# A fused linear-attention and MLP kernel on one core: GpSimd work moved out of the first group, rstd of later groups computed on VectorE, first loads regrouped

## Chip, cores, metric

One core of one Trainium2 chip. The metric is the device time of one execution in microseconds (us); lower is better. "Span" is the time from the first to the last instruction in one profiled execution; it is about 1.7 us below the time of that execution (217.1 against 218.81 us before the change). Engine names in profile lines: PE is TensorE (products), PEld its weight loads, DVE is VectorE, ACT is ScalarE, POOL is GpSimd, SP starts the loads. The granted clock is the share of the full TensorE clock that the profile shows as granted; 1.00 is full.

## The reference

```python
xn  = layernorm(x)                       # x: 2048 tokens x 640, bf16, eps 1e-5
q,k,v = split(xn @ wqkv)                 # 32 heads of 20
pq,pk = phi(q), phi(k)                   # phi(t) = where(t>0, t+1, exp(t)) + 1e-6
kv, z = einsum(pk, v), sum(pk)           # per head
A = (pq @ kv) / (pq @ z + 1e-6) @ wo
B = gelu(xn @ w1 + b1) @ w2 + b2         # 1536 hidden
out = x + A + B
```

## The kernel before

The 2048 tokens are worked on as four groups of four tiles of 128. For each group the kernel makes K (4 tiles), Q (5 products of 128x512 each) and the MLP's hidden layer h (12 products of 128x512, with GELU on ScalarE). The transposes of the next group's normalised tiles stand between the last h products. After the last group come the attention sums and, from about 140 us on, one long run of output products. The instruction order is the written order.

All products take their result space from one rotating pool of eight PSUM banks. A bank comes free only when ScalarE or VectorE has read it. So a late reader stops TensorE eight banks later: in the profile below the sixth, seventh and eighth h products, eight banks after the last three Q tiles, wait 0.33, 1.10 and 1.06 us for VectorE.

```python
def emit_rstd(t0, t1):                   # on ScalarE; profile before: no table load from 2.08 to 28.60 us
    r = rstd[:, t0:t1]
    nc.scalar.activation(out=r, in_=mv[:, t0:t1, 1], func=ACT.Ln, bias=eps_t[:], scale=1.0)
    nc.scalar.activation(out=r, in_=r, func=ACT.Exp, scale=-0.5)

def phi(dst, ps, shaped):                # every K and Q tile goes through this
    e = etmp.tile([P, TOK], BF16, name="e")
    nc.scalar.activation(out=e[:], in_=ps[:], func=ACT.Exp)
    nc.vector.tensor_scalar(out=e[:], in0=e[:], scalar1=1.0, scalar2=1e-6, op0=ALU.min, op1=ALU.add)   # "clamp"
    nc.vector.scalar_tensor_tensor(out=dst, in0=shaped(ps), scalar=0.0, in1=shaped(e), op0=ALU.max, op1=ALU.add)

# ... in emit_Kphi, when the fourth K tile of group g is done:
            for u in range(max(1, g * TPG), (g + 1) * TPG):        # GpSimd sums K over the tokens
                nc.gpsimd.tensor_tensor(out=..., in0=..., in1=pk[:, u, :], op=ALU.add)
            if g == 0:
                emit_masks()                                       # GpSimd builds constant masks
# ...
nc.vector.tensor_copy(out=b1col[:], in_=b1_bf[:])                  # the "b1 cast"
for g in range(NG):
    if g > 0:
        nc.scalar.preload_act_table_set("natural_log_exp_and_others")
        for i in range(TPG): emit_K(g * TPG + i)
    for m in range(NC):
        if g == 0 and m > 0:
            emit_stats(TPG + m - 1)                                # statistics of group 1
        emit_Q(g, m)
    if g < NG - 1:
        emit_rstd((g + 1) * TPG, (g + 2) * TPG)
        for j in range(NJ):                                        # NJ = 12
            emit_h(g, j)
            if 4 <= j < 8:  emit_norm((g + 1) * TPG + j - 4)
            if 8 <= j < 12:
                emit_T((g + 1) * TPG + j - 8, on_act=NC)           # transposes of group g+1
                if g < NG - 2:
                    emit_stats((g + 2) * TPG + j - 8)              # statistics two groups ahead
```

Of the kernel before, what the change touches and what calls it, by code (L numbers as in the profile page):

```python
# [9 lines left out]
ALU = mybir.AluOpType  # L10
BF16 = mybir.dt.bfloat16
F32 = mybir.dt.float32


@with_exitstack
def kernel(
# [12 lines left out]
    nc = tc.nc  # L29
    P = nc.NUM_PARTITIONS  # L30
# [3 lines left out]
    S, D = x2d.shape  # L34
# [3 lines left out]
    NT = S // P  # L38
    NC = D // P
    NJ = F // P  # L40
    TOK = 512
    NG = S // TOK
    TPG = TOK // P
    EPS = 1e-5
    HALF = D // 2
# [27 lines left out]
    zsum = GT[:, NC - 1, :]  # L73
# [13 lines left out]
    Em4 = consts.tile([P, D], BF16, name="Em4")  # L87
    ones = consts.tile([P, 1], BF16, name="ones")
    Z3t = consts.tile([P, NC, H], BF16, name="Z3t")
    eps_t = consts.tile([P, 1], F32, name="eps_t")  # L90
    recT = consts.tile([P, TOK], BF16, name="recT")
    warm = hT[0][:, 0, :]
# [2 lines left out]

    def bank(dtype=F32):
        return psum.tile([P, TOK if dtype == F32 else 2 * TOK], dtype, name="mm", tag="mm")
# [7 lines left out]
    def load_x(t0, t1):  # L105
        nc.sync.dma_start(out=x_all[:, t0:t1, :], in_=xv[:, t0:t1, :])  # L106

    load_x(0, 1)
    load_x(1, 2)
    load_x(2, 3)  # L110
    nc.sync.dma_start(out=wqk[:, :, D : 2 * D], in_=wqkv_v[:, :, D : 2 * D])
    load_x(3, 4)
    nc.sync.dma_start(out=wqk[:, :, 0:D], in_=wqkv_v[:, :, 0:D])
    load_x(4, 8)
    nc.sync.dma_start(out=w1[:], in_=w1_v)
# [54 lines left out]
    def emit_stats(t):  # L170
        emit_stats_half(t, 0)
        emit_stats_half(t, 1)

    def emit_rstd(t0, t1):
        r = rstd[:, t0:t1]
        nc.scalar.activation(out=r, in_=mv[:, t0:t1, 1], func=ACT.Ln, bias=eps_t[:], scale=1.0)
        nc.scalar.activation(out=r, in_=r, func=ACT.Exp, scale=-0.5)

    def emit_norm(t):
        nc.vector.tensor_scalar(  # L180
            out=xn[:, t, :], in0=x_all[:, t, :], scalar1=mv[:, t, 0:1], scalar2=rstd[:, t : t + 1],
            op0=ALU.subtract, op1=ALU.mult,
        )

    def emit_T(t, on_act):
        pT = bank(BF16)[:, 0:D].rearrange("p (c n) -> p c n", c=NC)
        for c in range(NC):
            nc.tensor.transpose(pT[:, c, :], xn[:, t, c * P : (c + 1) * P], identity[:])  # L188
        dst = xnT[:, :, t * P : (t + 1) * P]
        if on_act > 0:  # L190
            nc.scalar.copy(out=dst[:, 0:on_act, :], in_=pT[:, 0:on_act, :])
        if on_act < NC:
            nc.vector.tensor_copy(out=dst[:, on_act:NC, :], in_=pT[:, on_act:NC, :])

    def phi(dst, ps, shaped):
        e = etmp.tile([P, TOK], BF16, name="e")
# [9 lines left out]

    K_ps = {}

    def emit_Ka(t):
        K_ps[t] = bank()  # L210
        for k in range(NC):
            nc.tensor.matmul(  # L212
                K_ps[t][:], lhsT=xnT[:, k, t * P : (t + 1) * P], rhs=wqk[:, k, D : D + TOK],
                start=(k == 0), stop=(k == NC - 1),
            )

    def emit_Kb(t):
        g, i = divmod(t, TPG)
        if i == 0:
            rest_ps[g] = bank()  # L220
        for k in range(NC):
            nc.tensor.matmul(  # L222
                rest_ps[g][:, i * REST : (i + 1) * REST],
                lhsT=xnT[:, k, t * P : (t + 1) * P], rhs=wqk[:, k, D + TOK : 2 * D],
                start=(k == 0), stop=(k == NC - 1),
            )

    def emit_K(t):
        emit_Ka(t)
        emit_Kb(t)  # L230
        emit_Kphi(t)

    def emit_Kphi(t):
        g, i = divmod(t, TPG)
        phi(pk[:, t, 0:TOK], K_ps.pop(t), lambda a: a[:])
        if i == TPG - 1:
            phi(
                pk[:, g * TPG : (g + 1) * TPG, TOK:D], rest_ps[g],
                lambda a: a[:].rearrange("p (t n) -> p t n", t=TPG),
            )  # L240
            for u in range(max(1, g * TPG), (g + 1) * TPG):
                nc.gpsimd.tensor_tensor(  # L242
                    out=zsum if u == NT - 1 else zacc[:], in0=pk[:, 0, :] if u == 1 else zacc[:],
                    in1=pk[:, u, :], op=ALU.add,
                )
            if g == 0:
                emit_masks()

    def emit_Q(g, m):
        ps = bank()  # L250
# [18 lines left out]

    nc.scalar.preload_act_table_set("natural_log_exp_and_others")  # L270
    emit_warm(10)
    for t in range(2):
        emit_stats(t)
        emit_rstd(t, t + 1)
    emit_norm(0)
    emit_T(0, on_act=NC)
    emit_norm(1)
    emit_stats(2)
    emit_rstd(2, 3)
    emit_T(1, on_act=NC)  # L280
    emit_stats_half(3, 0)
    emit_norm(2)
    emit_stats_half(3, 1)
    emit_rstd(3, 4)
    emit_Ka(0)
    emit_Kb(0)
    emit_T(2, on_act=0)
    emit_norm(3)
    emit_Ka(1)
    emit_Kb(1)  # L290
    emit_T(3, on_act=NC)
    emit_Kphi(0)
    emit_Kphi(1)
    emit_K(2)
    emit_K(3)
    nc.vector.tensor_copy(out=b1col[:], in_=b1_bf[:])
    for g in range(NG):
        if g > 0:
            nc.scalar.preload_act_table_set("natural_log_exp_and_others")
            for i in range(TPG):  # L300
                emit_K(g * TPG + i)
        for m in range(NC):
            if g == 0 and m > 0:
                emit_stats(TPG + m - 1)
            emit_Q(g, m)
        if g < NG - 1:
            emit_rstd((g + 1) * TPG, (g + 2) * TPG)
            for j in range(NJ):
                emit_h(g, j)
                if 4 <= j < 4 + TPG:  # L310
                    emit_norm((g + 1) * TPG + j - 4)
                if 8 <= j < 8 + TPG:
                    emit_T((g + 1) * TPG + j - 8, on_act=NC)
                    if g < NG - 2:
                        emit_stats((g + 2) * TPG + j - 8)

    for t in range(NT):
        nc.gpsimd.tensor_tensor(out=x_all[:, t, :], in0=x_all[:, t, :], in1=b2b[:], op=ALU.add)  # L318
# [110 lines left out]
    for j in range(4 + NC, NJ):  # L429
        emit_h(NG - 1, j)  # L430

    for t in range(NT):
        g, i = divmod(t, TPG)
        osb = late[:, 2 * NC + t % 4, :]
        for half in range(2):
            ns = slice(half * HALF, (half + 1) * HALF)
            ps = bank()
            for j in range(NJ):
                nc.tensor.matmul(  # L439
                    ps[:, 0:HALF], lhsT=hT[g][:, j, i * P : (i + 1) * P], rhs=w2[:, j, ns],  # L440
                    start=(j == 0), stop=False,
                )
            for c in range(NC):
                nc.tensor.matmul(  # L444
                    ps[:, 0:HALF], lhsT=pqT[:, c, t * P : (t + 1) * P], rhs=KVW[:, c, ns],
                    start=False, stop=(c == NC - 1),
                )
            nc.vector.tensor_tensor(  # L448
                out=osb[:, ns], in0=ps[:, 0:HALF], in1=x_all[:, t, ns], op=ALU.add
            )  # L450
            if t == NT - 1:
                nc.sync.dma_start(out=ov[:, t, ns], in_=osb[:, ns])
        if t < NT - 1:
            nc.sync.dma_start(out=ov[:, t, :], in_=osb)


# [1 line left out]
_INS = ['A_x', 'A_wqkv', 'A_wo', 'B_x', 'B_w1', 'B_b1', 'B_w2', 'B_b2']  # L458
_OUTS = [((1, 2048, 640), 'bfloat16')]
# [25 lines left out]
```

## Time and profile before

Before the prediction six executions were known: median 219.07 us (218.57 to 220.85).

The page of the profiled execution begins with the span, the busy share of each engine, and the span in 40 slices of 5.4 us; a digit is the busy share in tenths. (Lines of the other engines are left out.)

```profile
span 217.1 us, 3343 instructions
...
PE 208.7 (96%) x1374; PEld 121.8 (56%) x1390; DVE 103.7 (48%) x212; ACT 82.1 (38%) x137; POOL 54.6 (25%) x59
...
PE   7899779999999999999999999999999999999994
...
DVE  4776995399719920595374425812212212112111
```

TensorE is busy nearly everywhere. The gap is in the fifth and sixth slice, 22 to 33 us, where VectorE is full. The timeline of TensorE (start, length, line, operation, operands, count; in brackets the idle time ahead of it and who ended it) shows this gap. Lines left out are busy ones.

```profile
7.37 1.24 PE L212 MATMUL mm<-wqk,xnT 128*128 128x512 bf16 x5 [0.55 <-DMA wqk<-in_A_wqkv_dram]
...
18.80 5.56 PE L262 MATMUL mm<-xnT,w_88 128*128 128x512 bf16 x24
24.69 1.24 PE L262 MATMUL mm<-xnT,w_88 128*128 128x512 bf16 x5 [0.33 <-DVE pqT L201]
27.04 1.24 PE L262 MATMUL mm<-xnT,w_88 128*128 128x512 bf16 x5 [1.10 <-DVE pqT L201]
29.33 2.54 PE L262 MATMUL mm<-xnT,w_88 128*128 128x512 bf16 x10 [1.06 <-DVE pqT L201]
...
36.07 1.24 PE L212 MATMUL mm<-wqk,xnT 128*128 128x512 bf16 x5
```

The first line starts the K products, after waiting 0.55 us for their weights. At 18.80 group 0's h products start. From 24.69 on they stop three times, each time for a bank that VectorE has not yet emptied (line 201 is the second half of phi). The last line is the first K product of group 1. Twelve h products of 1.08 us and four sets of transposes of 0.28 us (both as the chain of waits has them) need 14.08 us; 36.07 - 18.80 is 17.27. So group 0 loses 3.2 us here.

Why VectorE is late, from its own timeline in the same stretch, with ScalarE's and GpSimd's lines below:

```profile
18.55 1.34 DVE L296 CAST b1col<-b_bf 128x12 f32<-128x12 bf16 x1 [1.64 <-DMA b_bf<-in_B_b_dram]
...
20.72 0.88 DVE L166 BATCH_NORM_STATS2 stats<-x_all 128x6 f32<-128x320 bf16 x2
...
25.59 0.66 DVE L198 TENSOR_SCALAR e<-e 128x512 bf16<-128x512 bf16 x1
...
28.59 0.69 DVE L201 SCALAR_TENSOR_TENSOR pqT<-mm,e 128x512 bf16<-128x512 f32 x1
```

```profile
28.05 0.30 ACT L176 ACTIVATE rstd<-mv,eps_t 128x4 f32<-128x4 f32 x1 [4.64 <-DVE mv L168]
...
28.60 1.28 ACT L266 ACT_TABLE_LOAD   x1
29.90 5.31 ACT L266 ACTIVATE hT_80<-mm,b1col 128x512 bf16<-128x512 f32 x9
```

```profile
18.46 2.88 POOL L242 TENSOR_TENSOR zacc<-zacc,pk 128x640 f32<-128x640 f32 x2
```

VectorE waits for b1, then its tiny cast takes 1.34 us: it starts after a GpSimd add (1.40 us each) has begun at 18.46 and ends, at 19.89, as that add ends (19.86). Between Q tiles stand two statistics instructions per tile. A clamp beside GpSimd takes 0.66 us, one alone 0.28. GELU, which frees the first h banks, can start only at 29.90, because rstd and a table load of 1.28 us stand ahead of it.

### The profile page before, as it was taken

Reading aid. Unit: us, or ns where it says so; the run is one execution under the profiler, and the core shown is the slowest. Engines: PE = TensorE matmul, PEld = TensorE weight load, DVE = VectorE, ACT = ScalarE, POOL = GpSimd, SP = SyncE. Lnnn points to the kernel's source line nnn. Section 1 sums busy time; section 2 is a strip of 40 time slices with the busy share of each in tenths; the row PEclk is TensorE's granted clock in tenths of the full one; section 3 lists DMA queues with packets and bytes.
Section 4 is the critical chain, followed back from the end, with each engine's and each line's share of the span. In section 5 each row is a group of like instructions: output and inputs, shape, how many; then the busy total and the mean of one; then the engine's idle time right before and its main releaser. Section 6 shows DMA issues by size and latency. Waiting matters only on the chain.

```text
span 217.1 us, 3343 instructions
## 1 busy us (share of the span) xinstructions
PE 208.7 (96%) x1374; PEld 121.8 (56%) x1390; DVE 103.7 (48%) x212; ACT 82.1 (38%) x137; POOL 54.6 (25%) x59
## 2 busy tenths in 40 slices
PE   7899779999999999999999999999999999999994
PEld 2554335544554445545555565477777777777772
DVE  4776995399719920595374425812212212112111
ACT  3472189959796868751112646500000000000000
POOL 1008860045002700069999800000000000000000
PEclk9999999999999999999999999999999999999999
DMA  5999960000000000000000000001000010010011
GB/s 175 384 363 314 371 239 0 3 2 0 0 3 0 0 0 3 0 0 2 3 0 0 3 2 0 3 18 42 33 30 30 30 63 30 30 33 30 30 63 30
DMA packets 9999, 12.83 MB, mean 59 GB/s; under 512 B 2048, under 2 KB 8960, under 8 KB 9984
## 3 DMA queue, kind: packets, MB, share of 16 engines
q1 hardware_dynamic: 9984, 12.62, 17.1%
q8 instruction: 11, 0.18, 0.4%
q14 instruction: 4, 0.03, 0.0%
HBM read 10.00 MB, written 2.62 MB: 58 GB/s over the span
## 4 chain that ended last, share of the span: by engine, by line
PE 84%; DMA 6%; DVE 5%; SPq 2%; ACT 1%; issue 1%
PE mm L439 24%; PE mm L262 20%; PE mm L444 10%; PE mm L326 8%; PE mm L253 7%; DMA b_bf<-in_B_b_dram 6%; PE mm L212 6%; PE mm L335 2%; PE mm L418 2%; PE mm L222 2%; PE mm L188 2%; DVE stats L166 1%; DVE pqT L201 1%; SPq L106 1%; PE mm L374 1%
## 5 line engine op out<-in xcount | busy, mean ns | idle before, releaser
L262 PE MATMUL mm<-xnT,w_88 128*128 128x512 bf16 x232 | 54.8, 379 | 3.0 <-DVE pqT L201 2.5
L448 DVE TENSOR_TENSOR late<-mm,x_all 128x320 bf16<-128x320 f32 x32 | 15.7, 491 | 58.7 <-PE mm L444 58.7
L262 PEld LDWEIGHTS <-w_88 128*128 128x128 bf16 x240 | 22.8, 98 | 28.8 <-issue 4.1
L242 POOL TENSOR_TENSOR zacc<-zacc,pk 128x640 f32<-128x640 f32 x13 | 18.2, 1398 | 52.4 <-DVE pk L201 51.6
L198 DVE TENSOR_SCALAR e<-e 128x512 bf16<-128x512 bf16 x40 | 18.7, 467 | 24.9 <-ACT e L197 24.9
L197 ACT ACTIVATE e<-mm 128x512 bf16<-128x512 f32 x40 | 23.0, 597 | 15.7 <-DVE pqT L201 5.9
L444 PE MATMUL mm<-late,pqT 128*128 128x320 bf16 x160 | 27.0, 299 | 0.0
L253 PE MATMUL mm<-xnT,wqk 128*128 128x512 bf16 x98 | 22.1, 379 | 0.1
L318 POOL TENSOR_TENSOR x_all<-x_all,b2b 128x640 bf16<-128x640 bf16 x16 | 21.8, 1397 | 0.0
L212 PE MATMUL mm<-wqk,xnT 128*128 128x512 bf16 x77 | 19.6, 379 | 0.7 <-DMA wqk<-in_A_wqkv_dram 0.6
L444 PEld LDWEIGHTS <-pqT 128*128 128x128 bf16 x160 | 15.7, 98 | 6.1
L326 PE MATMUL mm<-pk,xn 128*128 128x512 bf16 x77 | 17.8, 379 | 0.3 <-issue 0.2
L253 PEld LDWEIGHTS <-wqk 128*128 128x128 bf16 x100 | 9.6, 98 | 10.9
L379 DVE TENSOR_TENSOR pqT<-pqT,mm 128x512 bf16<-128x512 bf16 x20 | 12.3, 680 | 6.0 <-PE mm L374 6.0
L166 DVE BATCH_NORM_STATS2 stats<-x_all 128x6 f32<-128x320 bf16 x32 | 13.8, 471 | 2.4 <-DMA x_all<-in_A_x_dram 2.4
L439 PE MATMUL mm<-w_90,hT_82 128*128 128x320 bf16 x96 | 14.3, 299 | 0.0
L439 PE MATMUL mm<-w_90,hT_80 128*128 128x320 bf16 x96 | 14.3, 299 | 0.0
L439 PE MATMUL mm<-w_90,hT_81 128*128 128x320 bf16 x96 | 14.3, 299 | 0.0
L439 PE MATMUL mm<-w_90,hT_1112 128*128 128x320 bf16 x96 | 14.3, 299 | 0.0
L201 DVE SCALAR_TENSOR_TENSOR pk<-mm,e 128x512 bf16<-128x512 f32 x20 | 13.8, 692 | 1.0
L201 DVE SCALAR_TENSOR_TENSOR pqT<-mm,e 128x512 bf16<-128x512 f32 x20 | 13.8, 692 | 0.7
L326 PEld LDWEIGHTS <-xn 128*128 128x128 bf16 x80 | 7.5, 98 | 9.2 <-issue 0.7
(62 smaller groups left out, 198.0 us busy)
## 6 DMA issues: line engine op xcount, KB each, us to landing
out_dram<-late SPq DMA_DIRECT2D x15, 160.0 KB, 1.8
x_all<-in_A_x_dram SPq DMA_DIRECT2D x3, 640.0 KB, 8.4
w_88<-in_B_w_dram SPq DMA_DIRECT2D x1, 1920.0 KB, 13.4
w_90<-in_B_w_dram SPq DMA_DIRECT2D x1, 1920.0 KB, 14.0
wqk<-in_A_wqkv_dram SPq DMA_DIRECT2D x2, 800.0 KB, 6.2
wv<-in_A_wqkv_dram SPq DMA_DIRECT2D x1, 800.0 KB, 9.0
wo<-in_A_wo_dram SPq DMA_DIRECT2D x1, 800.0 KB, 10.5
x_all<-in_A_x_dram SPq DMA_DIRECT2D x4, 160.0 KB, 2.9
```

The lines of the kernel that those rows point to most:

```text
L166: nc.vector.bn_stats(out=st[:, half, :], in_=x_all[:, t, half * HALF : (half + 1) * HALF])
L197: nc.scalar.activation(out=e[:], in_=ps[:], func=ACT.Exp)
L198: nc.vector.tensor_scalar(out=e[:], in0=e[:], scalar1=1.0, scalar2=1e-6, op0=ALU.min, op1=ALU.add)
L201: nc.vector.scalar_tensor_tensor(out=dst, in0=shaped(ps), scalar=0.0, in1=shaped(e), op0=ALU.max, op1=ALU.add)
L212: nc.tensor.matmul(K_ps[t][:], lhsT=xnT[:, k, t * P : (t + 1) * P], rhs=wqk[:, k, D : D + TOK], start=(k == 0), stop=(k == NC - 1),)
L242: nc.gpsimd.tensor_tensor(out=zsum if u == NT - 1 else zacc[:], in0=pk[:, 0, :] if u == 1 else zacc[:], in1=pk[:, u, :], op=ALU.add,)
L253: nc.tensor.matmul(ps[:], lhsT=wqk[:, k, m * P : (m + 1) * P], rhs=xnT[:, k, gs], start=(k == 0), stop=(k == NC - 1),)
L262: nc.tensor.matmul(ps[:], lhsT=w1[:, k, j * P : (j + 1) * P], rhs=xnT[:, k, g * TOK : (g + 1) * TOK], start=(k == 0), stop=(k == NC - 1),)
L318: nc.gpsimd.tensor_tensor(out=x_all[:, t, :], in0=x_all[:, t, :], in1=b2b[:], op=ALU.add)
L326: nc.tensor.matmul(ps[:], lhsT=w, rhs=pk[:, t, 0:TOK], start=(t == 0), stop=(t == NT - 1))
L439: nc.tensor.matmul(ps[:, 0:HALF], lhsT=hT[g][:, j, i * P : (i + 1) * P], rhs=w2[:, j, ns], start=(j == 0), stop=False,)
L444: nc.tensor.matmul(ps[:, 0:HALF], lhsT=pqT[:, c, t * P : (t + 1) * P], rhs=KVW[:, c, ns], start=False, stop=(c == NC - 1),)
```

## The change

The intent was to empty the Q banks of group 0 sooner and to start GELU sooner: no GpSimd work beside VectorE in group 0; the statistics moved behind the Q tiles; rstd of later groups on VectorE, as a Newton iteration on integers and floats, so that GELU's table load need not wait for it; and an earlier start.

```diff
+    def load_wk(k0, k1): ...                       # K weights in two loads
     load_x(0, 1)
-    load_x(1, 2)
-    load_x(2, 3)
-    nc.sync.dma_start(out=wqk[:, :, D : 2 * D], in_=wqkv_v[:, :, D : 2 * D])
-    load_x(3, 4)
+    load_x(1, 4)
+    load_wk(0, 2)
+    load_wk(2, NC)
...
+    def emit_rstd_vector(t0, t1):                  # 13 instructions on 128x4 elements
+        v = mv[...] + EPS; a = v >> 1; y = 0x5F3759DF - a; v = -0.5 * v      # (shortened)
+        for _ in range(3):
+            nc.vector.tensor_tensor(out=a, in0=v, in1=y, op=ALU.mult)
+            nc.vector.tensor_tensor(out=a, in0=a, in1=y, op=ALU.mult)
+            nc.vector.scalar_tensor_tensor(out=y, in0=a, scalar=1.5, in1=y, op0=ALU.add, op1=ALU.mult)
...
-    for t in range(2):
-        emit_stats(t)
-        emit_rstd(t, t + 1)
-    emit_norm(0)
-    emit_T(0, on_act=NC)
+    emit_stats(0)
+    emit_rstd(0, 1)
+    emit_stats_half(1, 0)                          # ahead of norm 0
+    emit_norm(0)
+    emit_T(0, nc.scalar.copy, 0, 3)                # tile 0 in two parts
+    emit_stats_half(1, 1)
+    emit_rstd(1, 2)
+    emit_T(0, nc.scalar.copy, 3, NC)
...
         for m in range(NC):
-            if g == 0 and m > 0:
-                emit_stats(TPG + m - 1)
             emit_Q(g, m)
-        if g < NG - 1:
-            emit_rstd((g + 1) * TPG, (g + 2) * TPG)
-            for j in range(NJ):
-                emit_h(g, j)
-                if 4 <= j < 4 + TPG:
-                    emit_norm((g + 1) * TPG + j - 4)
-                if 8 <= j < 8 + TPG:
-                    emit_T((g + 1) * TPG + j - 8, on_act=NC)
-                    if g < NG - 2:
-                        emit_stats((g + 2) * TPG + j - 8)
+        for j in range(NJ if g < NG - 1 else 0):
+            emit_h(g, j)
+            if g == 0 and j == NJ - 1:             # GpSimd held by a copy that needs the last GELU
+                nc.gpsimd.tensor_copy(out=Z3t[:, 0, 0:1], in_=hT[0][:, j, 0:1])
+                emit_zacc(0)
+                emit_masks()
+            if j < TPG:
+                emit_stats(t1 + j)                 # statistics of the NEXT group, in every group
+            if j == TPG:
+                emit_rstd_vector(t1, t1 + TPG)
+            if TPG <= j < 2 * TPG:
+                emit_norm(t1 + j - TPG)
+            if j > 2 * TPG:
+                emit_T(t1 + j - 2 * TPG - 1, nc.scalar.copy)
+            if j == NJ - 1:
+                emit_T(t1 + TPG - 1, nc.scalar.copy)
...      # the last output piece is cut into 512 and 128 columns instead of 320 and 320
```

More of the change, by code (lines that the diff above doesn't have):

```diff
@@ L12 @@
 F32 = mybir.dt.float32
+I32 = mybir.dt.int32
 @with_exitstack
@@ L89 @@
     Z3t = consts.tile([P, NC, H], BF16, name="Z3t")
+    newton = consts.tile([P, 2, TPG], F32, name="newton")
     eps_t = consts.tile([P, 1], F32, name="eps_t")
@@ L106, in load_x, with load_wk @@
         nc.sync.dma_start(out=x_all[:, t0:t1, :], in_=xv[:, t0:t1, :])
+    def load_wk(k0, k1):
+        nc.sync.dma_start(out=wqk[:, k0:k1, D : 2 * D], in_=wqkv_v[:, k0:k1, D : 2 * D])
     load_x(0, 1)
-    load_x(1, 2)
-    load_x(2, 3)
-    nc.sync.dma_start(out=wqk[:, :, D : 2 * D], in_=wqkv_v[:, :, D : 2 * D])
-    load_x(3, 4)
+    load_x(1, 4)
+    load_wk(0, 2)
+    load_wk(2, NC)
     nc.sync.dma_start(out=wqk[:, :, 0:D], in_=wqkv_v[:, :, 0:D])
@@ L177, in emit_rstd, with emit_norm, emit_T @@
         nc.scalar.activation(out=r, in_=r, func=ACT.Exp, scale=-0.5)
-    def emit_norm(t):
-        nc.vector.tensor_scalar(
-            out=xn[:, t, :], in0=x_all[:, t, :], scalar1=mv[:, t, 0:1], scalar2=rstd[:, t : t + 1],
+    def emit_rstd_vector(t0, t1):
+        n = t1 - t0
+        y = rstd[:, t0:t1]
+        v, a = newton[:, 0, 0:n], newton[:, 1, 0:n]
+        nc.vector.tensor_scalar(out=v, in0=mv[:, t0:t1, 1], scalar1=EPS, scalar2=None, op0=ALU.add)
+        nc.vector.tensor_scalar(
+            out=a.bitcast(I32), in0=v.bitcast(I32), scalar1=1, scalar2=None,
+            op0=ALU.logical_shift_right,
+        )
+        nc.vector.tensor_scalar(
+            out=y.bitcast(I32), in0=a.bitcast(I32), scalar1=-1.0, scalar2=float(0x5F3759DF),
+            op0=ALU.mult, op1=ALU.add,
+        )
+        nc.vector.tensor_scalar(out=v, in0=v, scalar1=-0.5, scalar2=None, op0=ALU.mult)
+        for _ in range(3):
+            nc.vector.tensor_tensor(out=a, in0=v, in1=y, op=ALU.mult)
+            nc.vector.tensor_tensor(out=a, in0=a, in1=y, op=ALU.mult)
+            nc.vector.scalar_tensor_tensor(
+                out=y, in0=a, scalar=1.5, in1=y, op0=ALU.add, op1=ALU.mult
+            )
+    def emit_norm(t, c0=0, c1=NC):
+        ds = slice(c0 * P, c1 * P)
+        nc.vector.tensor_scalar(
+            out=xn[:, t, ds], in0=x_all[:, t, ds], scalar1=mv[:, t, 0:1], scalar2=rstd[:, t : t + 1],
             op0=ALU.subtract, op1=ALU.mult,
         )
-    def emit_T(t, on_act):
-        pT = bank(BF16)[:, 0:D].rearrange("p (c n) -> p c n", c=NC)
-        for c in range(NC):
-            nc.tensor.transpose(pT[:, c, :], xn[:, t, c * P : (c + 1) * P], identity[:])
-        dst = xnT[:, :, t * P : (t + 1) * P]
-        if on_act > 0:
-            nc.scalar.copy(out=dst[:, 0:on_act, :], in_=pT[:, 0:on_act, :])
-        if on_act < NC:
-            nc.vector.tensor_copy(out=dst[:, on_act:NC, :], in_=pT[:, on_act:NC, :])
+    def emit_T(t, copy, c0=0, c1=NC):
+        n = c1 - c0
+        pT = bank(BF16)[:, 0 : n * P].rearrange("p (c n) -> p c n", c=n)
+        for c in range(n):
+            nc.tensor.transpose(pT[:, c, :], xn[:, t, (c0 + c) * P : (c0 + c + 1) * P], identity[:])
+        copy(out=xnT[:, c0:c1, t * P : (t + 1) * P], in_=pT)
     def phi(dst, ps, shaped):
@@ L207, with emit_Ka @@
     K_ps = {}
-    def emit_Ka(t):
-        K_ps[t] = bank()
-        for k in range(NC):
+    def emit_Ka(t, k0=0, k1=NC):
+        if k0 == 0:
+            K_ps[t] = bank()
+        for k in range(k0, k1):
             nc.tensor.matmul(
@@ L240, in emit_Kphi, with emit_zacc @@
             )
-            for u in range(max(1, g * TPG), (g + 1) * TPG):
-                nc.gpsimd.tensor_tensor(
-                    out=zsum if u == NT - 1 else zacc[:], in0=pk[:, 0, :] if u == 1 else zacc[:],
-                    in1=pk[:, u, :], op=ALU.add,
-                )
-            if g == 0:
-                emit_masks()
+            if g > 0:
+                emit_zacc(g)
+    def emit_zacc(g):
+        for u in range(max(1, g * TPG), (g + 1) * TPG):
+            nc.gpsimd.tensor_tensor(
+                out=zsum if u == NT - 1 else zacc[:], in0=pk[:, 0, :] if u == 1 else zacc[:],
+                in1=pk[:, u, :], op=ALU.add,
+            )
     def emit_Q(g, m):
@@ L271 @@
     emit_warm(10)
-    for t in range(2):
-        emit_stats(t)
-        emit_rstd(t, t + 1)
+    emit_stats(0)
+    emit_rstd(0, 1)
+    emit_stats_half(1, 0)
     emit_norm(0)
-    emit_T(0, on_act=NC)
-    emit_norm(1)
+    emit_T(0, nc.scalar.copy, 0, 3)
+    emit_stats_half(1, 1)
+    emit_rstd(1, 2)
+    emit_T(0, nc.scalar.copy, 3, NC)
     emit_stats(2)
     emit_rstd(2, 3)
-    emit_T(1, on_act=NC)
+    emit_norm(1)
+    emit_Ka(0, 0, 4)
+    emit_T(1, nc.scalar.copy)
+    emit_Ka(0, 4, NC)
+    emit_Kb(0)
     emit_stats_half(3, 0)
@@ L284 @@
     emit_rstd(3, 4)
-    emit_Ka(0)
-    emit_Kb(0)
-    emit_T(2, on_act=0)
-    emit_norm(3)
+    emit_T(2, nc.vector.tensor_copy)
     emit_Ka(1)
     emit_Kb(1)
-    emit_T(3, on_act=NC)
+    emit_norm(3)
+    emit_T(3, nc.scalar.copy)
     emit_Kphi(0)
@@ L297 @@
     for g in range(NG):
+        t0, t1 = g * TPG, (g + 1) * TPG
         if g > 0:
@@ L300 @@
             for i in range(TPG):
-                emit_K(g * TPG + i)
+                emit_K(t0 + i)
         for m in range(NC):
-            if g == 0 and m > 0:
-                emit_stats(TPG + m - 1)
             emit_Q(g, m)
-        if g < NG - 1:
-            emit_rstd((g + 1) * TPG, (g + 2) * TPG)
-            for j in range(NJ):
-                emit_h(g, j)
-                if 4 <= j < 4 + TPG:
-                    emit_norm((g + 1) * TPG + j - 4)
-                if 8 <= j < 8 + TPG:
-                    emit_T((g + 1) * TPG + j - 8, on_act=NC)
-                    if g < NG - 2:
-                        emit_stats((g + 2) * TPG + j - 8)
+        for j in range(NJ if g < NG - 1 else 0):
[14 more added lines that the diff above has]
+                emit_T(t1 + TPG - 1, nc.scalar.copy)
     for t in range(NT):
@@ L430, with emit_out @@
         emit_h(NG - 1, j)
+    def emit_out(t, ns, osb):
+        g, i = divmod(t, TPG)
+        ps = bank()[:, 0 : ns.stop - ns.start]
+        for j in range(NJ):
+            nc.tensor.matmul(
+                ps, lhsT=hT[g][:, j, i * P : (i + 1) * P], rhs=w2[:, j, ns], start=(j == 0), stop=False
+            )
+        for c in range(NC):
+            nc.tensor.matmul(
+                ps, lhsT=pqT[:, c, t * P : (t + 1) * P], rhs=KVW[:, c, ns],
+                start=False, stop=(c == NC - 1),
+            )
+        nc.vector.tensor_tensor(out=osb[:, ns], in0=ps, in1=x_all[:, t, ns], op=ALU.add)
     for t in range(NT):
-        g, i = divmod(t, TPG)
         osb = late[:, 2 * NC + t % 4, :]
-        for half in range(2):
-            ns = slice(half * HALF, (half + 1) * HALF)
-            ps = bank()
-            for j in range(NJ):
-                nc.tensor.matmul(
-                    ps[:, 0:HALF], lhsT=hT[g][:, j, i * P : (i + 1) * P], rhs=w2[:, j, ns],
-                    start=(j == 0), stop=False,
-                )
-            for c in range(NC):
-                nc.tensor.matmul(
-                    ps[:, 0:HALF], lhsT=pqT[:, c, t * P : (t + 1) * P], rhs=KVW[:, c, ns],
-                    start=False, stop=(c == NC - 1),
-                )
-            nc.vector.tensor_tensor(
-                out=osb[:, ns], in0=ps[:, 0:HALF], in1=x_all[:, t, ns], op=ALU.add
-            )
-            if t == NT - 1:
+        if t < NT - 1:
+            emit_out(t, slice(0, HALF), osb)
+            emit_out(t, slice(HALF, D), osb)
+            nc.sync.dma_start(out=ov[:, t, :], in_=osb)
+        else:
+            for ns in (slice(0, TOK), slice(TOK, D)):
+                emit_out(t, ns, osb)
                 nc.sync.dma_start(out=ov[:, t, ns], in_=osb[:, ns])
-        if t < NT - 1:
-            nc.sync.dma_start(out=ov[:, t, :], in_=osb)
 _INS = ['A_x', 'A_wqkv', 'A_wo', 'B_x', 'B_w1', 'B_b1', 'B_w2', 'B_b2']
```

## The prediction

> **What bounds the kernel.** TensorE: 96% busy (page); 73.9 of 73.9 us from 140.2 on, 15.95 of 16 in 41 to 57 (busy time by windows). A 128x512 product takes 0.216 us in sequence (chain of waits: x5 in 1.08). Two idle places are worth taking: 0.55 us at 7.4 (K weights), and about 3.3 us between 24.3 and 30.6. There, group 0's MLP product runs out of PSUM banks: the timeline shows VectorE waiting until 18.55 for b1, its tiny cast taking 1.34 us beside a GpSimd add (1.40), then each Q tile costing 0.93 plus 1.04 of statistics, with e-clamps of 0.66 instead of 0.28 beside GpSimd; rstd on ScalarE ends at 28.6, then a 1.28 table load, first GELU 29.9.
>
> **Group 0 after.** No GpSimd, no statistics between Q tiles, no rstd before the table load: Q drains in 5 x 0.925 = 4.6 us after b1, by about 23; GELU starts near 22.5; the bank stalls go. What limits then is VectorE: 4 statistics x 1.03, Newton, a norm of 0.4. Newton is 13 tiny instructions, 12 dependent. [...] 160 elements 0.32 us, 512 elements 0.69, so 0.15 at none. With 0.03 handover between dependent ones I estimate 0.19 each, 2.4 us. The first transpose is ready near 29.7 to 30.1; PE wants it at about 29.5. K of group 1 starts at 32.9 to 33.4 instead of 36.23: gain 2.8 to 3.3.
>
> **Loads.** Early loads are limited by issue (about 0.45 us each; 170 GB/s at 3 to 4 us); fewer, larger ones land everything, b1 included, perhaps 0.5 us earlier. But half of tile 1's statistics now stands ahead of norm 0 and waits for a 480 KB load, so K tile 2 starts about where it did (10.7). Worth 0 to 0.5, mostly hidden behind VectorE's chain.
>
> **Group 1.** GpSimd's adds (3 x 1.4) and masks (9.5 us) now run from about 33 to 47.5, then group 1's adds (5.8) to about 53. [...] e-clamps take 0.83 beside adds, 0.28 alone. So group 1's Newton chain begins inside these adds, advancing a step or two per 1.46 us; its first transpose is ready about 22.7 us after K starts, where PE wants it at 21.6. New stall 1.1 us (0 to 1.8). Group 2: 0 to 0.3. After that unchanged.
>
> **End.** The last piece has 128 columns: its add falls from 0.49 to about 0.29, the final store shrinks: 0.2 to 0.3 gained; PE work equal.
>
> **Sum.** -3.1 - 0.2 - 0.25 + 1.1 + 0.15 = -2.3: **216.8 us**, range 215.2 to 218.1. Faster by over 2% (below 214.7) 6%, within 2% 93%, slower 1%.
>
> **What would show it.** Right: no PE gap at 24 to 31; first GELU near 22.5; idle PE before the first transposes of groups 1 and 2, VectorE the releaser; Newton steps about 0.16 each in group 0, over 1 us in places in group 1. Wrong: no idle there.
>
> **What would make it wrong.** Newton cheaper or not excluded by GpSimd (near 215.3); masks slowed further by VectorE (group 1 stalls 2 us or more); K weights late, moving the whole start.

The 0.15 us at no elements, and with it the 0.29 of the last add, is a straight line through the two figures beside it. The 0.03 is the gap that dependent VectorE instructions show there (a clamp ends at 12.41, the next instruction starts at 12.44). That GpSimd would hold Newton is read from the b1 cast (1.34 us) and the clamps (0.83) beside its adds of 1.40 to 1.46 us. That early loads are limited by issue is the reading of the first eight issues, 0.37 to 0.58 us each, and of 170 GB/s from 3 to 4 us, where 384 to 410 came at 8 to 10.

## The result, and the profile after

The changed kernel took 218.03 us (median of 20 runs, 217.45 to 220.01), the kernel before 219.14 us (40 runs, 218.09 to 220.89). The ratio is 0.9956, 95% interval 0.9936 to 0.9976. Ratios here are the mean time of one kernel's runs over that of the other's of the same rounds, so they are not quite the ratio of the medians quoted. So the change is clear of noise and a little under half as large as forecast: 1.1 us instead of 2.3.

The head of the page after, as before:

```profile
span 216.3 us, 3378 instructions
...
PE 208.1 (96%) x1373; PEld 120.8 (56%) x1390; DVE 108.3 (50%) x251; ACT 82.4 (38%) x132; POOL 55.4 (26%) x60
...
PE   7799999999799999999999999999999999999994
```

The dark slice around 22 to 33 us is gone, and a fainter one (the eleventh slice, from 54 us) is new. TensorE's timeline:

```profile
6.89 0.60 PE L236 MATMUL mm<-wqk,xnT 128*128 128x512 bf16 x2 [0.46 <-ACT xnT L216]
7.93 0.59 PE L236 MATMUL mm<-wqk,xnT 128*128 128x512 bf16 x2 [0.43 <-DMA wqk<-in_A_wqkv_dram]
...
19.34 10.96 PE L288 MATMUL mm<-xnT,w_88 128*128 128x512 bf16 x49
...
33.41 1.24 PE L236 MATMUL mm<-wqk,xnT 128*128 128x512 bf16 x5
...
56.71 0.45 PE L215 MATMUL mm<-identity,xn 128*128 128x128 bf16 x5 [1.51 <-DVE xn L206]
...
59.99 1.24 PE L236 MATMUL mm<-wqk,xnT 128*128 128x512 bf16 x5
...
82.09 0.45 PE L215 MATMUL mm<-identity,xn 128*128 128x128 bf16 x5 [0.31 <-DVE xn L206]
```

Group 0's h products (19.34) now run without a stop, and K of group 1 starts at 33.41: 14.07 us, no more than the sum above gives (14.08). But in front of group 1's first transposes (56.71) TensorE idles 1.51 us, in front of group 2's (82.09) 0.31, both for VectorE's norm. And the start is split: the first two K products at 6.89, then a wait for the second K load to 7.93. ScalarE's table load and first GELU come at:

```profile
20.79 1.28 ACT L292 ACT_TABLE_LOAD   x1
22.08 2.47 ACT L292 ACTIVATE hT_80<-mm,b1col 128x512 bf16<-128x512 f32 x4
```

VectorE's timeline: the b1 cast alone, two Newton steps of group 0, then one clamp of group 1's Q tiles held beside a mask (46.88 to 47.60), group 1's first three Newton instructions and its norms; below it GpSimd's adds of group 1.

```profile
18.05 0.17 DVE L326 CAST b1col<-b_bf 128x12 f32<-128x12 bf16 x1 [0.61 <-DMA b_bf<-in_B_b_dram]
...
27.59 0.16 DVE L198 TENSOR_TENSOR newton<-newton,rstd 128x4 f32<-128x4 f32 x1
27.78 0.16 DVE L199 TENSOR_TENSOR newton<-newton,rstd 128x4 f32<-128x4 f32 x1
...
46.90 0.85 DVE L221 TENSOR_SCALAR e<-e 128x512 bf16<-128x512 bf16 x1
...
52.52 0.32 DVE L187 TENSOR_SCALAR newton<-mv 128x4 f32<-128x4 f32 x1
52.88 0.17 DVE L188 TENSOR_SCALAR newton<-newton 128x4 int32<-128x4 int32 x1
53.08 1.25 DVE L192 TENSOR_SCALAR rstd<-newton 128x4 int32<-128x4 int32 x1
...
56.20 1.51 DVE L206 TENSOR_SCALAR xn<-x_all,mv,rstd 128x640 bf16<-128x640 bf16 x4
```

```profile
48.47 5.84 POOL L270 TENSOR_TENSOR zacc<-zacc,pk 128x640 f32<-128x640 f32 x4
```

In group 0 a Newton instruction takes 0.16 to 0.17 us and a dependent one starts 0.19 to 0.21 us after the one ahead of it. In group 1 the chain starts at 52.5, inside the adds. One instruction takes 1.25 us and ends (54.33) as the last add ends (54.31); after that the rest take 0.16 us each.

Reading the first K product of each group as a milestone gives a table that separates what the total mixes. (Where the trace lacks the first product, the milestone is the end of the transposes ahead of it, 0.28 us per tile.)

| stage on TensorE, us | before | after | difference |
|---|---|---|---|
| start of h, group 0 | 18.80 | 19.34 | +0.54 |
| h of group 0 to K of group 1 | 17.27 | 14.07 | -3.20 |
| K of group 1 to K of group 2 | 24.89 | 26.58 | +1.69 |
| K of group 2 to K of group 3 | 24.90 | 25.38 | +0.48 |
| K of group 3 to the last product's end | 128.25 | 128.26 | 0 |
| from there to the end | 2.99 | 2.67 | -0.32 |
| span | 217.1 | 216.3 | -0.8 |

So 2.66 us were won by the time K of group 1 starts, and 2.17 us were given back in groups 1 and 2. (The stall of group 1 counts 1.69 here and 1.51 in the profile's wait, because the profile's modelled end of a product lies about 0.16 us behind the point where the next could have started: five products last 1.24 us in the timeline and 1.08 in sequence.)

The wait list of TensorE has these waits in one line, as waits in total, times, longest; the third wait in it is 0.51 us for norm 0 at the start:

```profile
PE mm L215 <- DVE xn L206: 2.3, 3, 1.5
```

### The profile page after: what moved, and what is told of

It is laid out like the page before. It is cut to its first block, busy times and chain, and to the rows that moved or that the text cites. A ratio compares the mean times of both kernels' runs of the same rounds, so it can differ in the third digit from the quotient of the medians.

```text
span 216.3 us, 3378 instructions
## 1 busy us (share of the span) xinstructions
PE 208.1 (96%) x1373; PEld 120.8 (56%) x1390; DVE 108.3 (50%) x251; ACT 82.4 (38%) x132; POOL 55.4 (26%) x60
## 4 chain that ended last, share of the span: by engine, by line
PE 73%; DVE 17%; ACT 3%; DMA 3%; issue 2%; SPq 1%; DVEq 0%
PE mm L471 24%; PE mm L288 14%; PE mm L475 10%; PE mm L361 8%; PE mm L279 5%; DVE e L221 4%; PE mm L236 4%; DVE pqT L224 3%; DVE pk L224 3%; DVE stats L170 3%; DMA wqk<-in_A_wqkv_dram 3%; PE mm L370 2%; PE mm L453 2%; PE mm L215 2%; ACT L330 1%
## 5 line engine op out<-in xcount | busy, mean ns | idle before, releaser
L288 PE MATMUL mm<-xnT,w_88 128*128 128x512 bf16 x232 | 53.7, 379 | 0.4
L479 DVE TENSOR_TENSOR late<-mm,x_all 128x320 bf16<-128x320 f32 (+2 forms) x32 | 15.7, 492 | 58.5 <-PE mm L475 58.5
L221 DVE TENSOR_SCALAR e<-e 128x512 bf16<-128x512 bf16 x40 | 18.0, 450 | 19.6 <-ACT e L220 19.6
L475 PE MATMUL mm<-late,pqT 128*128 128x320 bf16 (+2 forms) x160 | 27.0, 299 | 0.0
L471 PE MATMUL mm<-w_90,hT_81 128*128 128x320 bf16 x96 | 14.3, 299 | 0.0
L471 PE MATMUL mm<-w_90,hT_80 128*128 128x320 bf16 x96 | 14.3, 299 | 0.0
L471 PE MATMUL mm<-w_90,hT_82 128*128 128x320 bf16 x96 | 14.3, 299 | 0.0
L471 PE MATMUL mm<-w_90,hT_1148 128*128 128x320 bf16 (+2 forms) x95 | 14.3, 298 | 0.1
```

The source lines that it names most:

```text
L288: nc.tensor.matmul(ps[:], lhsT=w1[:, k, j * P : (j + 1) * P], rhs=xnT[:, k, g * TOK : (g + 1) * TOK], start=(k == 0), stop=(k == NC - 1),)
L471: nc.tensor.matmul(ps, lhsT=hT[g][:, j, i * P : (i + 1) * P], rhs=w2[:, j, ns], start=(j == 0), stop=False)
L475: nc.tensor.matmul(ps, lhsT=pqT[:, c, t * P : (t + 1) * P], rhs=KVW[:, c, ns], start=False, stop=(c == NC - 1),)
```

## The experiments

Theory after the result: the statistics and rstd of groups 1 and 2 used to be ready a group ahead. The change put them, as a serial chain, between the last Q tile and the first norm; this chain is longer than the h products that cover it, and GpSimd's moved work lengthens it further in group 1. Rivals: the loss is GpSimd's hold alone; or it is the number of Newton steps alone; or the regrouped loads cost the missing time. Each run lists the ratio to the kernel before in the same rounds. Stages are read as in the table above. All the kernels gave correct results.

### Start as before the change

```diff
 # changed kernel
     load_x(0, 1)
-    load_x(1, 4)
-    load_wk(0, 2)
-    load_wk(2, NC)
+    load_x(1, 2)
+    load_x(2, 3)
+    load_wk(0, NC)
+    load_x(3, 4)
... # and the old instruction order from emit_stats(0) up to emit_T(3)
```

> The changed kernel with the loads and the instruction order of the first group's start as before the change. In the changed kernel group 0's MLP product starts at 19.34 us, before the change at 18.80, because the second part of the K weights landed at 7.9. Theory: the lost 0.54 us comes back at that point (18.8), but nearly nothing of it survives, because b1 lands 0.5 us later again (18.55), and VectorE's chain (Q tiles, statistics, Newton, norm) then ends at about 30.3, where PE wants the first transpose at 29.6; K of group 1 starts within 0.25 us of the changed kernel's 33.41, and the time is the same within 0.25 us. Rival: the late K weights are a plain loss on TensorE's path; K of group 1 starts at 32.9 and the kernel is 0.5 us faster than the changed one.

Measured: 218.57 us (4 runs), ratio 0.9972 (0.9908 to 1.0037). Both expectations failed on the same point. The K weights landed later than in the kernel before with the same loads: the first K product started at 8.54 us, h of group 0 at 19.96, K of group 1 at 34.24, which is 0.83 us behind the changed kernel. What held was the second half of the theory: VectorE's b1 cast came at 19.14, its first norm at 30.45, and the stage from h to K of group 1 grew to 14.28, so its chain was just binding. The lesson was that one profile of the start is not a measurement of it. The first K product with the old start came at 7.4, 8.5 and 8.9 us in three profiles.

### GpSimd alone

```diff
 # kernel before
-            for u in ...: nc.gpsimd.tensor_tensor(...)      # group 0's adds
-            if g == 0: emit_masks()
+                if g == 0 and j == NJ - 1:                  # behind the last GELU, as in the change
+                    nc.gpsimd.tensor_copy(out=Z3t[:, 0, 0:1], in_=hT[0][:, j, 0:1])
+                    emit_zacc(0)
+                    emit_masks()
```

> The kernel before with one part of the change: GpSimd's adds of group 0 and the masks moved behind the last GELU of group 0; nothing else. Theory: GpSimd being away makes up about half of group 0's gain. The b1 cast takes 0.17 instead of 1.34 us, clamps 0.28; Q tiles with a tile of statistics between them still cost 1.96 us each, last Q tile done near 27.5 (29.3 before), first GELU near 28.5 (29.9). PE idles 1.7 us instead of 3.3 between 24 and 31. No new stall in groups 1 and 2, as statistics and rstd stay ahead. Time 1.6 us below before (ratio 0.993), that is at or below the whole change. Rival: GpSimd matters little and the gain of group 0 came from moving statistics and rstd; then under 0.5 us.

Measured: 218.22 us (4 runs), ratio 0.9931 (0.9869 to 0.9994), in the direction of the theory. But three of the four executions, the profiled one too, ran with a mean granted clock of 0.992. In this profile the clock is low only up to 11.9 us. After that, h of group 0 starts at 21.73, 2.9 us later than in the profile of the kernel before, and runs to K of group 1 in 14.06 us with no bank stall. As the late start also gave VectorE more time, this run can't tell how much of the stall GpSimd's move alone removes. This execution showed something else. The K weights were late, and the windows view (stretch, length, busy time of PE, PEld, DVE, ACT, POOL, granted clock, DMA share, GB/s) gives:

```profile
6.50:8.50 2.00, 0.28 (x5) 0.20 (x3) 0.77 (x3) 1.35 (x4) 0.00 (x0) 0.99 1.03 355
8.50:11.50 3.00, 2.60 (x10) 1.22 (x10) 1.45 (x4) 0.50 (x2) 0.00 (x0) 0.50 1.05 410
11.50:14.00 2.50, 2.50 (x25) 1.72 (x23) 0.85 (x2) 0.18 (x1) 0.00 (x0) 0.92 1.03 402
```

```profile
8.90 2.29 PE L212 MATMUL mm<-wqk,xnT 128*128 128x512 bf16 x5 [2.13 <-DMA wqk<-in_A_wqkv_dram]
```

After 2.13 us of waiting the granted clock is 0.50 for about 3.4 us, from 8.46 to 11.88 (worked out from windows of 0.5 us: the mean clock is 0.96 from 8.0 to 8.5 and 0.62 from 11.5 to 12.0, with 0.50 in all between; an expectation further down quotes this stretch as 8.3 to 11.7). That is the second thing that came with the late start in this execution. Between the last dummy product's end (5.45) and the first K product (8.90) lie only transposes and idling. But a fixed limit for the wait does not come out of the profiles. Here the clock fell 3.0 us after the last dummy product, in "The new start alone" about 2.5 us after it (4.92 to about 7.4, with single waits of no more than 1.48 us), and in "GpSimd put back" 3.5 us after the last h product (29.96 to about 33.5); each of the three dips lasted about 3.4 us, by the mean clocks of the windows. In "Start as before the change" 3.58 us without an ordinary product (4.96 to 8.54), again with only transposes and idling in them, brought no dip at all (clock 1.00 in every window from 0 to 50 us). What decides between these cases, and whether the transposes matter, is not shown by any run.

### GpSimd put back

```diff
 # changed kernel
+            emit_zacc(g)                # in emit_Kphi, for every group
+            if g == 0: emit_masks()
-            if g == 0 and j == NJ - 1: ...
```

> The changed kernel with GpSimd's adds of group 0 and the masks put back where they were before (from 17 us). Theory: Newton in group 0 now runs beside the masks, so the first transpose of group 0 comes at about 33 instead of 30 us: PE idles about 3 us there. In group 1 the adds are over before Newton starts, so its stall shrinks from 1.69 us to about 0.5, as in group 2. Net 2.0 us slower than the changed kernel. Rival: if GpSimd does not hold up the small Newton steps, group 0 stalls under 1 us and the kernel is as fast as the changed one or faster.

Measured: 221.94 us (4 runs; one of them, 223.37, is over 1.5% above the fastest and is not in the ratio), ratio 1.008 (1.0003 to 1.0156), and 220.02 in the one execution at full clock. Group 0's first transposes waited 2.83 us (32.79 instead of about 29.8), group 1's stage fell to 25.40: both as the theory has it. Newton is only a part of that wait. Three of its instructions were held for 0.57 to 0.66 us beside the masks, so that it took 3.7 us instead of 2.4; but the chain also began 1.6 us later (28.52 instead of 26.90), because the b1 cast (1.14 us) and two clamps (0.76 and 1.03) were held beside GpSimd's work. After the long wait the clock was 0.52 from 33.5 to 37.0 us in this profile. The rival is out: GpSimd does hold the small Newton instructions (0.57 to 0.66 us instead of 0.16 to 0.17).

### Two Newton steps instead of three

```diff
-        for _ in range(3):
+        for _ in range(2):
```

> The changed kernel with two Newton steps instead of three (three instructions fewer, 0.59 us shorter by the trace). Theory: VectorE's chain before the first transpose is on TensorE's path in groups 1 and 2 only. Group 1's stall falls by 0.6 (1.69 to 1.1), group 2's of 0.47 goes; group 0 does not move (its transposes were 0.3 us early). Time 1.0 to 1.1 us below the changed kernel. Rival: the returned time is GpSimd's hold alone, then under 0.3 us.

Measured: 216.81 us, ratio 0.9890 (0.9830 to 0.9951), 1.2 us below the changed kernel's median, in different rounds. Stages: 14.07, 25.99, 24.90. Three instructions fewer took 0.59 us out of group 1 and the whole 0.48 out of group 2; group 0 did not move. So it is the chain's length that counts there, and the result was still correct.

### Statistics one group earlier

```diff
-            if j < TPG:
+            if g == 0 and j < TPG:
                 emit_stats(t1 + j)
+            if g < NG - 2 and 2 * TPG <= j:
+                emit_stats(t1 + TPG + j - 2 * TPG)
```

> The changed kernel with the statistics of groups 2 and 3 taken one group earlier, behind the norms at the end of the MLP product, where VectorE is idle (30.9 to 36.9 us), as before the change; three Newton steps, in their place. Stage lengths on TensorE, read as starts: K of group 1 to K of group 2 was 24.89 us before the change and 26.58 after, K of group 2 to K of group 3 24.90 and 25.38. Theory (what counts is the length of VectorE's chain in front of the first transpose, and GpSimd's adds hold Newton): group 2's loss of 0.48 goes altogether (24.9). In group 1 Newton now starts at about 48.4 and runs through the four adds of 1.46 us, two or three steps per add, to about 55: stage about 25.5, 1.0 us gained of 1.69. Sum 1.5 us below the changed kernel. Rival (GpSimd's hold on Newton does not matter, only the chain's length): both stages 24.9, 2.2 us below.

Measured: 216.49 us, ratio 0.9876 (0.9833 to 0.9919). Stages: 14.07, 25.75, 24.89; the theory had 25.5 and 24.9, the rival 24.9 twice. Newton in group 1 now lies fully beside the four adds (48.13 to 53.98):

```profile
48.06 0.16 DVE L187 TENSOR_SCALAR newton<-mv 128x4 f32<-128x4 f32 x1
48.25 1.31 DVE L188 TENSOR_SCALAR newton<-newton 128x4 int32<-128x4 int32 x1
49.59 0.17 DVE L192 TENSOR_SCALAR rstd<-newton 128x4 int32<-128x4 int32 x1
49.67 1.38 DVE L196 TENSOR_SCALAR newton<-newton 128x4 f32<-128x4 f32 x1
51.08 0.16 DVE L198 TENSOR_TENSOR newton<-newton,rstd 128x4 f32<-128x4 f32 x1
51.28 1.25 DVE L199 TENSOR_TENSOR newton<-newton,rstd 128x4 f32<-128x4 f32 x1
```

Every second instruction takes 1.25 to 1.38 us and ends as an add ends (49.56, 51.05, 52.53 and 54.01; at 1.46 us each the adds end at 49.59, 51.06, 52.52 and 53.98); the one behind it slips through in 0.16 to 0.17. Four of thirteen are held, the integer shift (1.31 us) like the float ones. So the rate beside the adds was two small instructions per add.

### Group 1's adds later

```diff
-            if g > 0: emit_zacc(g)
+            if g > 1: emit_zacc(g)
...
+            if g == 1 and j == NJ - 1:
+                nc.gpsimd.tensor_copy(out=Z3t[:, 0, 0:1], in_=hT[1][:, j, 0:1])
+                emit_zacc(1)
```

> The changed kernel with GpSimd's four adds of group 1 held until group 1's last GELU, so that they are not beside group 1's Newton steps. Theory: Newton takes 2.45 us instead of 3.68, so the stage K of group 1 to K of group 2 falls by 1.2 us, from 26.58 to about 25.4. The adds then run beside K's clamps of group 2 and delay VectorE's chain there by about 1.1 us: the next stage grows from 25.38 to about 26.4. Sum nearly zero (0.3 us either way). Rival (the hold costs nothing): both stages unchanged.

Measured: 217.62 us, ratio 0.9928 (0.9889 to 0.9967). Stages: 14.06, 25.27, 26.42, where 25.4 and about 26.4 were expected. The hold on Newton is worth 1.3 us in group 1, and the same adds cost 1.0 us when they stand beside the clamps of group 2. Against the changed kernel the medians differ by 0.4 us, in different rounds.

### Statistics and a two-step Newton one group ahead

```diff
 # the edits of "Statistics one group earlier" and "Two Newton steps", and
-            if j == TPG:
+            if g == 0 and j == TPG:
                 emit_rstd_vector(t1, t1 + TPG)
+            if g < NG - 2 and j == NJ - 1:
+                emit_rstd_vector(t1 + TPG, t1 + 2 * TPG)
```

> Meant to beat both: the changed kernel with statistics and a two-step Newton of groups 2 and 3 both taken one group ahead, in VectorE's idle time; group 0 as in the changed kernel but with two steps. Theory: no first transpose waits for VectorE; stages 24.9 and 24.9, group 0 as in the changed kernel (start of the MLP product to K of group 1 14.07). 2.2 us below the changed kernel, about 215.8 in an execution at full clock, ratio to before 0.983 to 0.987. If the adds and masks beside it hold Newton past the K clamps of the next group, a part of this is lost, but no more than 0.5.

Measured: 215.67 us (6 runs), ratio 0.9845 (0.9803 to 0.9886). Stages: 14.07, 24.89, 24.90. No transposes wait for VectorE in the later groups; of TensorE's waits only those at the start and one of 0.2 us are left:

```profile
PE mm L159 <- DVE hT L128: 1.3, 1, 1.3
PE mm L215 <- DVE xn L206: 0.8, 1, 0.8
PE mm L236 <- ACT xnT L216: 0.5, 1, 0.5
PE mm L365 <- issue: 0.2, 1, 0.2
```

(Line 215 here is tile 0's transpose at 6.26 us.) Newton beside GpSimd's adds of group 0 was still held three times, 1.25 to 1.37 us each, but where nothing waited for it.

### The new start alone

```diff
 # kernel before
     load_x(0, 1)
-    load_x(1, 2)
-    load_x(2, 3)
-    nc.sync.dma_start(out=wqk[:, :, D : 2 * D], in_=wqkv_v[:, :, D : 2 * D])
-    load_x(3, 4)
+    load_x(1, 4)
+    load_wk(0, 2)
+    load_wk(2, NC)
... # and the changed instruction order from emit_stats(0) up to emit_T(3)
```

> The kernel before with one part of the change: the regrouped first loads and the order of the first group's start. In three profiles with the old start the first K product began at 7.4, 8.5 and 8.9 us, in three with the new one K went on without a gap after 7.9, 7.0 and 7.6 us. Theory: the new start is earlier in most executions, by 0.5 us or more, and idles TensorE less, so that fewer executions show a granted clock under 1; b1 lands earlier and the GELU of group 0 starts up to 1 us earlier. 0.4 to 1.0 us below before. Rival (as the first pair of profiles reads): the second K load lands late, and the new start costs 0.5 us or is worth nothing because group 0's MLP product waits for VectorE anyway.

Measured: 218.66 us against 219.18, ratio 0.9969 (0.9938 to 0.9999): 0.5 us, at the low end of what was expected. One of six executions had a clock of 0.992, against six of eleven of the kernel before in these rounds. The profiled execution was that one: tile 0's transposes waited 1.48 us for norm 0.

```profile
6.41 0.45 PE L192 MATMUL mm<-identity,xn 128*128 128x128 bf16 x5 [1.48 <-DVE xn L183]
```

In the new order half of tile 1's statistics stands ahead of norm 0. In two other profiles of the new start it waited for the load of tiles 1 to 3 until 0.90 us ahead of these transposes (5.08 of 5.98, 5.36 of 6.26 us); here that would be 5.51 us, an estimate from those. Then the clock fell: its mean was 0.93 from 4 to 8 us, 0.65 from 8 to 12 and 1.00 after that, which with 0.50 in the dip puts it at about 7.4 to 10.8. So the new start has a late load of its own to wait for.

### Dummy products while the K weights are awaited

```diff
 # kernel before
     emit_rstd(3, 4)
+    emit_warm(6)
     emit_Ka(0)
```

> The kernel before with six dummy 128x512 products (1.3 us) behind the second transpose, where TensorE otherwise waits for the K weights with nothing to do. So far 10 of 18 executions of the kernel before had a mean granted clock of 0.992 or less, and 4 of 21 of the changed one; in the one such profile of the old start the clock is 0.5 from 8.3 to 11.7 us, right after 2.1 us of waiting for the K weights. Theory: idle TensorE at the start brings the dip, so with the filler at most one or two of six executions show a clock under 0.995, and the spread of times shrinks; median about 218.9, as the full-clock executions of before. Rival: the dips come from the bank stalls at 24 to 31 us; then about half of the executions still show them.

Measured: 219.38 us against 218.79 in the same rounds, ratio 1.0012 (0.9986 to 1.0037). All six executions ran at clock 1.000, while six of eleven of the kernel before in the same rounds had 0.992 or less. The bank stalls were still there in this profile (1.7 us of waiting at 27 to 30 us). With six executions this speaks for the start as what brings the clock dips, and against the bank stalls. "GpSimd alone" points the same way: its profile has no bank stall, and three of its four executions dipped. The median, expected near 218.9, came out higher; in the profile the K products started at 8.74 and group 0's stage still took 16.54 us. In these runs the filler bought an even clock, not time.

### New start and GpSimd moved, no Newton

```diff
 # kernel before, with both edits: "The new start alone" and "GpSimd alone"
+    load_x(1, 4); load_wk(0, 2); load_wk(2, NC)    # and the order, as above
-            if g == 0: emit_masks()
+                if g == 0 and j == NJ - 1: ...; emit_zacc(0); emit_masks()
```

> The kernel before with two parts of the change, the new start and GpSimd still in group 0; statistics between the Q tiles and rstd on ScalarE as before, no Newton. Theory: Q tiles end at about 27.0, rstd at 26.6, GELU starts at about 28.0 instead of 29.9; TensorE idles about 0.8 us in group 0, so K of group 1 starts at about 34.2 (changed kernel 33.41), but the stages of groups 1 and 2 stay at 24.9 (26.58 and 25.38 in the changed kernel). So it ends 1.3 us before the changed kernel, near 216.9 with the old, unsplit last piece: the Newton steps and the late statistics, though they win 0.8 us in group 0, lose more than they win. Rival: without the Newton part group 0 stalls by 2 us or more and the time is that of the changed kernel or above.

Measured: 216.37 us (6 runs), ratio 0.9887 (0.9859 to 0.9915). This run separates the change best:

```profile
18.96 10.18 PE L265 MATMUL mm<-xnT,w 128*128 128x512 bf16 x44
...
33.34 1.24 PE L213 MATMUL mm<-wqk,xnT 128*128 128x512 bf16 x5
```

```profile
27.17 5.31 ACT L269 ACTIVATE hT<-mm,b1col 128x512 bf16<-128x512 f32 x9
```

With statistics still between the Q tiles and rstd still on ScalarE, GELU starts at 27.17, K of group 1 at 33.34 (expected 34.2; the changed kernel 33.41), after a stage of 14.38, which is 0.3 above the 14.08 of the sum. Groups 1 and 2 take 24.89 and 24.90. It came out better than expected; one reason that the profile shows is b1, which landed at 17.40 us in this execution (18.05 in the changed kernel's profile). So moving GpSimd, with the new start, removes nearly all of the bank stall; the Newton part adds only the last 0.3 us of that stage.

### Norm 0 first

```diff
 # the best kernel so far
-    emit_stats_half(1, 0)
     emit_norm(0)
+    emit_stats_half(1, 0)
```

> The best kernel so far (statistics and a two-step Newton one group ahead, 215.67) with norm 0 ahead of the first half of tile 1's statistics, so that tile 0's transposes do not wait for the 480 KB load of tiles 1 to 3. Theory from the prediction: the first transposes start at about 5.5 instead of 6.26, the first K products at about 6.4 instead of 7.17; what remains is then the wait for the second K load (7.0 to 7.9), so K of tile 2 starts 0 to 0.5 us earlier than 11.10 and the time falls by 0 to 0.4. Rival: the start is bound by the K load alone and nothing moves.

Measured: 215.69 us (6 runs, all at clock 0.999 or 1.000), ratio 0.9841 (0.9816 to 0.9866): the same as without it. The first transposes started at 5.50 and the first K products at 6.59, and then TensorE waited for the second K load until 7.98; K of tile 2 came at 11.29. The rival holds: the time did not move, and with norm 0 out of the way the start waited for the K load.

### Clock dips over all runs

Counting executions with a mean granted clock of 0.992 or less: kernel before, 16 of the 29 beside these experiments; changed kernel, 4 of 21; the seven other kernels with the new start, leaving out the one with GpSimd put back and its long wait, 2 of 36. The kernel before has a median of 218.82 us in its 13 full-clock executions and 219.55 in its 16 others; the changed kernel 217.89 (17) and 219.65 (4). At full clock the change is therefore worth 0.93 us, close to the 0.8 us of the spans. The rest of its 1.1 us is probably fewer dips; that was not tested by itself.

## Why the prediction was wrong

- **What bounds the kernel** was right: TensorE, with one gap in group 0 worth 3.2 us. So was the size of the change as a class: within 2%.
- **Group 0** ("K of group 1 starts at 32.9 to 33.4 instead of 36.23: gain 2.8 to 3.3") was right in mechanism: first GELU at 22.08 (22.5 forecast), Newton 0.16 each, no stall. The gain was 2.66, just under that range. (36.23 is 0.16 us above the 36.07 of the timeline, which does not touch the gain.) What bound the stage was not VectorE, as forecast, but TensorE itself, since h started 0.54 us later: VectorE's first norm was done at about 29.8, and TensorE got there at 30.13.
- **Loads** ("worth 0 to 0.5") was counted as -0.2. In the first pair of profiles it was +0.54, because the second K load landed at 7.93. But the old start itself varies: its first K product came between 7.37 and 8.90 us, and the profile that the forecast was read from had an early one. Over six executions the new start is worth 0.3% (0.9969, with an interval up to 0.9999), probably in part through fewer clock dips, which the prediction did not consider at all.
- **Group 1** ("New stall 1.1 us (0 to 1.8)") is the term that was mis-sized most: 1.69. The chain was forecast to be ready 22.7 us after K starts and came at 23.3, against a need at 21.6. GpSimd's masks ended at 48.4 us instead of 47.5 and group 1's adds at 54.3 instead of about 53. The Q tiles ended only 15.0 us after K, because four clamps were held: one beside an add (0.76 us) and three beside the masks (0.84 to 0.86), where one alone takes 0.28. These holds come to about 2.2 us (an estimate from these figures); for group 1 the prediction names only Newton as held. Newton then met only the last two adds and took 3.7 us. The hold on Newton as such was as forecast; the run with the adds moved away gives it 1.3 us. How the missing 0.6 us divides between the clamps and Newton stays open.
- **Group 2** ("0 to 0.3", counted 0.15) was 0.48. Two sets of transposes now stand behind the last h product, both copies stand in ScalarE's queue ahead of the table load, and the clamps of group 2 begin 3.45 us after K instead of 3.13. That 0.3 us lies on a chain that had no slack left; it was not tested by itself.
- **End** ("0.2 to 0.3") was 0.32.

The terms as forecast: -3.3 for group 0 and loads, +1.25 for groups 1 and 2, -0.25 for the end. As measured in the pair of profiles: -2.66, +2.17, -0.32. So two steps of the prediction failed, in size and not in mechanism. The stall that VectorE's chain puts ahead of the first transposes of groups 1 and 2 was taken as 1.1 and 0.15 us and measured 1.69 and 0.48, 0.9 us more. And the gain up to K of group 1 was taken as 3.3 us with the loads and measured 2.66, 0.6 us less, because h began 0.54 us later behind the second K load. A chain that is placed with no slack turns every small misjudgement into time. Here each chain was forecast to end at or after the moment TensorE wants it (in group 0, "ready near 29.7 to 30.1; PE wants it at about 29.5"), and these errors had the same sign.

Where the gain went is settled by the ratios to the kernel before: new start 0.9969; with GpSimd moved 0.9887; with the Newton part and the split last piece 0.9956. The Newton part, with the late statistics, costs 0.7%, and K of group 1 starts no earlier with it (33.41) than without (33.34; there h began 0.38 us earlier and took 0.31 longer). It is the place that costs, not Newton as such: one group ahead, with two steps, the ratio was 0.9845, with the split last piece in it. Not settled: why the K weights land up to 1.5 us (7.37 to 8.90) and b1 up to 0.6 us (casts that waited for it at 18.55 and 19.14 with the old start) earlier or later from one execution to the next, with the same loads in front of them.

## What to carry to other kernels

When work is moved to relieve one stage, follow it to where it lands: compare the length of the serial chain there, not its busy time, with the work that covers it, and leave slack. Preparation that used to run one stage ahead in idle time should stay there. Before a multi-part change is kept, take each part alone: here two of the three parts made the gain and the third, where it stood, gave more than half of it back.
